# A fused attention, expert and feed-forward kernel: the order of its attention part is changed

## The chip, the cores and the metric

The kernel runs on one core of a Trainium2 chip. The metric is the device time of one execution in microseconds (us); lower is better. Engines are named as in the profile: PE (TensorE matmul) and PEld (its weight load), DVE (VectorE), ACT (ScalarE), POOL (GpSimd), SP (SyncE, which here only issues transfers). A name with a q behind it (ACTq, SPq) is the engine's instruction queue: issuing a transfer shows there.

## What is computed

Three stages follow one another: a decayed linear attention over 2 sequences of 768 tokens (8 heads of 64), a mixture of 8 experts in which each of the 1536 tokens goes to the 2 best by a noisy gate, and a dense feed-forward with a softmax-like activation and a norm.

```python
# attention: q, k, v of (2, 8, 768, 64)
gamma = 1.0 - 2.0 ** (-5.0 - np.arange(H, dtype=np.float32))
for t in range(S):
    state = gamma[None, :, None, None] * state + np.einsum('bhd,bhe->bhde', k[:, :, t], v[:, :, t])
    y[:, :, t] = scale * np.einsum('bhd,bhde->bhe', q[:, :, t], state)
# experts: x of (1536, 512), 8 experts of 512 x 1024 x 512
logits = x @ w_gate
noise_scale = np.log1p(np.exp(x @ w_noise))
noisy_logits = logits + noise_scale * noise
top2 = np.argpartition(-noisy_logits, 2, axis=1)[:, :2]
for e in range(E):
    for k in range(2):
        mask = top2[:, k] == e
        h = np.maximum(x[mask] @ w1[e], 0.0)
        out[mask] += top2_w[mask, k, None] * (h @ w2[e])
# feed-forward: 512 -> 1024 -> 512
h = x @ w_in
solu = h * softmax(h)
ln = (solu - mu) / np.sqrt(var + 1e-06) * g_ln
return ln @ w_out
```

## The kernel before, in words

**Attention.** 12 tiles of 128 tokens, one a step (i = 0 to 11; tiles of the two sequences in turn). A step issues on PE: `from_state` (L407, the query against the running state), `kv` (L418, the state's update), `from_chunk` (L433, within the tile), `scores(i + 1)` (L390), and `rows_logits(i)` (L444: the tile's rows and its 16 gate columns, out of the tile's transposed result `xT`). DVE masks the scores (`pm`, L392), ACT copies out the state `S` (L422), `xT` (L435), the rows `x` (L448) and the logits (L449). POOL scales queries and values two steps ahead (`qs`, L374, and `vs`, L378). SP issues the loads of queries, keys and values three steps ahead (`load_qk`, `load_kv`: four of 256 KB a tile), the store of the rows to `xd` (256 KB, L450) and, in seven of the steps, a load of 512 KB of the first expert's weights (`feed`); `split_unit` turns these into two parts on ACT (L202) and DVE (L203).

**Choosing.** The tiles are chosen in groups of 4, 4, 2 and 2. `choose(g)`, driven by `route(g)`, is a chain of some 25 small DVE operations (L466 to L489) with one trip to ACT; its `chosen` (L481) and `cum` (L483) are what `rank(g)` multiplies on PE (L561, L562) to number the tokens of each expert. `first_rows` (L503 to L513) makes from it the list of the first expert's tokens; `slots` (L571 to L579) makes the places in the table `token_of`; `scatter(i)` writes tile i's token numbers there with two indirect transfers on POOL (L629, L630). All 24 of them must have landed before POOL reads the second expert's list (`load_xg(1)`, L899) and gathers its rows `xr` in four indirect transfers (L914).

**First expert.** `list_rows` and `first_xt` gather its rows directly. `hidden(0, f, ...)` (L645) first computes 192 tokens for f = 0 to 7, then, after `turns` (order of the experts, and the list addresses `at_r`, L593), the other 256. `second(0, j)` (L969) follows in four pieces of 24 matmuls; behind the first piece PE turns the second expert's rows (`xg_t(1, 0)`, L928), and so on. From there on PE works through the experts and the feed-forward.

**Order.** The order is written out by hand: each engine and each queue runs its instructions in the order of the program, and waits on semaphores at the head. At the start ACT's queue issues two loads (`dec`, `kt`), then eleven small transfers: zeros to the table, eight pieces of 64 partitions x 2 x 8 numbers of the gates, written straight into `unit` (L280), the noise in two (L284), `gcol` (L286); its first computation (`fade`, L352) stands behind them. The pools give three buffers each to the loaded tiles, to `qs`, `vs` and `x`.

Of the kernel before, what the change touches and what calls it, by code (L numbers as in the profile page):

```python
# [44 lines left out]
def retnet_moe_solu(ctx, tc, qT, kT, k, v, w_gate, w_noise, noise, w1, w2, w_in, w_out, g_ln,  # L45
# [195 lines left out]
    def load_kv(i):  # L241
        if i >= NT:
            return
        c, b = order[i]
        for src, dst, nm in ((v, VT, "vt"), (k, KN, "kn")):
            t = ld.tile([128, H, D], F32, tag=nm, name=nm)
            nc.sync.dma_start(t, src[b, c])
            dst[i] = t
# [3 lines left out]
    load_qk(0)  # L252
    load_kv(0)
# [16 lines left out]
    nc.scalar.dma_start(token_of[:E * ROOM].rearrange("(p n) o -> p (n o)", p=128), zero)  # L270
# [3 lines left out]
    gate_at = (slice(128, 128 + 2 * E), slice(0, 2 * E))  # L274
# [8 lines left out]
    for b in range(B):  # L283
# [53 lines left out]
    load_kv(2)  # L337


    rows = [bank("c2", (128, HP, 128)), bank("c3", (128, HP, 128))]  # L340
# [6 lines left out]
    for s in range(2):  # L347
# [6 lines left out]
    first = wk.tile([128, 128], F32, name="first", bufs=1)  # L354
    nc.vector.memset(first, 0.0)
    nc.vector.memset(first[0:1], math.sqrt(D))
    p = bank("a1", (128, NC, H))
    nc.tensor.matmul(p, first, dec[:, 1], start=True, stop=True)
    chunk = wk.tile([128, NC, HP], F32, name="chunk", bufs=1)
    for s in range(2):  # L360
        r = slice(64 * s, 64 * s + 64)
        nc.vector.tensor_copy(chunk[r], p[r, :, s::2])
# [5 lines left out]
    def scale_qv(i):  # L368
# [12 lines left out]
    def scores(i):  # L381
# [56 lines left out]
    def rows_logits(i):  # L438
        x = wk.tile([128, 2, 2, 2, D], F32, tag="x", name="x", bufs=3)
# [231 lines left out]
    for i in range(NT):  # L671
        load_qk(i + 3)
        load_kv(i + 3)
# [3 lines left out]
        from_chunk(i)  # L677
        if i == 10:
            list_rows(0, range(EARLY_TILES), "a0")
        scores(i + 1)  # L680
        if i == 5:
            rank(0, "a1")
        rows_logits(i)
        if i == 4:
            route(0)
# [5 lines left out]
        if i == 7:  # L691
            slots(0)
        if i == 8:
            route(1)
            route(1)
            scatter(0)
            rank(1, "a1")
        if i == 9:
            first_rows(1)
            scatter(1)  # L700
        if i == 10:
            route(1)
            slots(1)
            scatter(2)
            route(2)
        if i == 11:
            route(2)
            scatter(3)
            rank(2, "a1")
            first_xt(0, 0)  # L710
            route(2)
            first_xt(0, 2)
            first_rows(2)
        feed(max(0, min(i - 3, LEAD)), max(0, min(i - 1, LEAD + 3)))
# [527 lines left out]
```

## Time and profile before

| what | value |
|---|---|
| time of the runs | 571.66, 572.23, 574.74 us (median 572.23) |
| the profiled execution: its time, its span | 572.88 us, 570.9 us |
| PE busy | 516.4 us (90%) |
| DVE, ACT, POOL busy | 373.3, 216.8, 232.8 us |
| mean granted clock of TensorE | 0.952 |
| PE in 40 slices (tenths) | 7598578882999999999999999999799888999986 |
| PE's clock in 40 slices (tenths) | 9798895995999999999999999999989899999999 |

A slice is 14.3 us; a 9 means busy for 90% or more. The first ten slices hold the attention, the choosing and the first expert. A row of a timeline gives the start and the length in us, the engine, the line, the operation, the tile written and those read, and in brackets how long the engine had been idle and what released it. A length is that of one instruction, or from the first start to the last end where x counts more.

### The profile page before, as it was taken

The numbers are of one execution on the slowest core, as the hardware profiler recorded it, in microseconds if no ns is written. First come the engines' busy times: TensorE is split into PE (matmuls) and PEld (weight loads), VectorE is DVE, ScalarE is ACT, GpSimd is POOL, SyncE is SP. The second block draws the span as 40 slices with busy tenths as digits, with TensorE's granted clock in tenths as the row PEclk, the third lists the DMA queues.
The fourth block names the chain that finished last, engine by engine and source line by source line (L and its number), as shares of the span: only waits on it lengthen the run. The fifth ranks groups of instructions, "written<-read, shape, count | busy, mean of one in ns | idle before, by whom it ended". The sixth has DMA issues, their size and how long they took to land.

```text
span 570.9 us, 8942 instructions
## 1 busy us (share of the span) xinstructions
PE 516.4 (90%) x3211; PEld 467.4 (82%) x3211; DVE 373.3 (65%) x731; ACT 216.8 (38%) x430; POOL 232.8 (41%) x309
## 2 busy tenths in 40 slices
PE   7598578882999999999999999999799888999986
PEld 6587467881999899999999999998587767878776
DVE  4139665550777888698787988885357566565640
ACT  0565331331443243343433425434434443334431
POOL 3436540775666572460714500000423545553421
PEclk9798895995999999999999999999989899999999
DMA  6699722205866668587686775758433553555331
GB/s 230 168 301 351 275 69 90 75 2 166 282 214 184 210 212 280 159 232 235 211 215 217 184 264 182 209 150 235 141 101 71 170 148 121 162 144 158 99 95 58
DMA packets 60514, 100.88 MB, mean 177 GB/s; under 512 B 11024, under 2 KB 28528, under 8 KB 60464
## 3 DMA queue, kind: packets, MB, share of 16 engines
q1 hardware_dynamic: 49680, 84.30, 47.2%
q0 software_dynamic: 6592, 15.54, 9.4%
q10 hardware_dynamic: 4192, 0.41, 0.5%
q8 instruction: 27, 0.44, 0.3%
q14 instruction: 23, 0.19, 0.1%
HBM read 77.52 MB, written 22.70 MB: 176 GB/s over the span
## 4 chain that ended last, share of the span: by engine, by line
PE 52%; DVE 12%; DMA 5%; ACT 4%; issue 3%; POOL 0%; SPq 0%; POOLq 0%; ACTq 0%; DVEq 0%
PE c L969 18%; PE b L645 11%; PE a L645 11%; PE d L767 7%; PE b L854 4%; DVE z L786 2%; DVE ee L781 2%; DVE t L739 2%; ACT ee L780 1%; DVE st L772 1%; DMA wr<-w_out 1%; PE a L748 1%; DMA zc<-zd 1%; DVE wl L203 1%; DMA xr<-xd,rows 1%
## 5 line engine op out<-in xcount | busy, mean ns | idle before, releaser
L914 POOL DMA_INDIRECT xq<-xd,rows x78 | 85.4, 1095 | 61.8 <-issue 61.1
L203 DVE TENSOR_TENSOR wl<-wr,wh 128x1024 fp32r<-128x1024 f32 x68 | 81.8, 1220 | 2.5 <-ACT wh L202 2.4
L969 PE MATMUL c<-hh,wh 128*128 128x448 f32 (+5 forms) x224 | 79.9, 357 | 0.0
L969 PE MATMUL c<-hl,wh 128*128 128x448 f32 (+5 forms) x224 | 79.6, 355 | 0.0
L969 PE MATMUL c<-hh,wl 128*128 128x448 f32 (+5 forms) x224 | 79.5, 355 | 0.0
L202 ACT ACTIVATE wh<-wr 128x1024 fp32r<-128x1024 f32 x68 | 70.0, 1051 | 1.2 <-DMA wr<-in_moe_w_dram 1.2
L728 POOL DMA_INDIRECT y<-yg,slot_y x24 | 23.8, 993 | 91.4 <-DMA yg<-y 85.8
L645 PE MATMUL b<-xh,wh 128*128 128x192 f32 (+8 forms) x176 | 58.3, 341 | 2.8 <-DVE hl L648 1.3
L645 PE MATMUL b<-xh,wl 128*128 128x192 f32 (+8 forms) x176 | 57.3, 335 | 0.0
L844 POOL TENSOR_TENSOR zl<-zc,zh 128x1024 fp32r<-128x1024 f32 x10 | 24.2, 2422 | 50.1 <-ACT zh L843 50.1
L969 PEld LDWEIGHTS c<-hh,wh 128*128 128x128 f32 x224 | 42.8, 191 | 1.2
L969 PEld LDWEIGHTS c<-hh,wl 128*128 128x128 f32 x224 | 42.6, 190 | 1.2
L969 PEld LDWEIGHTS c<-hl,wh 128*128 128x128 f32 x224 | 42.6, 190 | 1.2
L767 PE MATMUL d<-wh,x2h 128*128 128x512 f32 x96 | 40.3, 420 | 1.5 <-ACT y L1034 1.5
L647 ACT ACTIVATE hh<-b 128x192 fp32r<-128x192 f32 (+8 forms) x44 | 20.0, 454 | 54.5 <-PE b L645 51.2
L854 PE MATMUL b<-wh,zh 128*128 128x512 f32 (+1 forms) x104 | 38.4, 375 | 1.5 <-ACT zh L843 1.5
L767 PE MATMUL d<-wh,x2l 128*128 128x512 f32 x96 | 39.4, 411 | 0.0
L767 PE MATMUL d<-wl,x2h 128*128 128x512 f32 x96 | 39.0, 407 | 0.0
L645 PEld LDWEIGHTS b<-xh,wh 128*128 128x128 f32 x176 | 35.4, 201 | 4.4 <-DVE hl L648 1.7
L645 PE MATMUL a<-xh,wh 128*128 128x448 f32 (+6 forms) x112 | 38.9, 348 | 0.0
L645 PE MATMUL a<-xh,wl 128*128 128x448 f32 (+6 forms) x112 | 38.8, 346 | 0.0
L854 PE MATMUL b<-wl,zh 128*128 128x512 f32 (+1 forms) x104 | 38.3, 374 | 0.0
(206 smaller groups left out, 1087.0 us busy)
## 6 DMA issues: line engine op xcount, KB each, us to landing
wr<-in_moe_w_dram SPq DMA_DIRECT2D x60, 512.0 KB, 5.6
zd<-zs SPq DMA_DIRECT2D x40, 128.0 KB, 2.3
zc<-zd SPq DMA_DIRECT2D x10, 512.0 KB, 4.2
raw<-in_moe_w_in_dram SPq DMA_DIRECT2D x8, 512.0 KB, 4.7
raw<-in_moe_w_out_dram SPq DMA_DIRECT2D x8, 512.0 KB, 4.8
yg<-yr SPq DMA_DIRECT2D x16, 208.0 KB, 3.8
qt<-in_qT_dram SPq DMA_DIRECT2D x12, 256.0 KB, 5.3
vt<-in_v_dram SPq DMA_DIRECT2D x12, 256.0 KB, 5.5
```

The source lines that it names most:

```text
L202: nc.scalar.activation(hi, t, AF.Copy)
L203: nc.vector.tensor_sub(lo, t, hi)
L645: nc.tensor.matmul(p, w[:, 0, f * 128:(f + 1) * 128], x[:, d, c], start=(n == 0), stop=(n == len(terms) - 1))
L647: nc.scalar.activation(hh[:, f, c], p, AF.Relu)
L728: nc.gpsimd.indirect_dma_start(out=t, out_offset=None, in_=yg[:upto], in_offset=bass.IndirectOffsetOnAxis(ap=slot_y[:, i, s:s + 1], axis=0))
L739: nc.vector.scalar_tensor_tensor(t, y1, top_w[:, i, 1:2], t, op0=OP.mult, op1=OP.add)
L767: nc.tensor.matmul(PH[i][:, s, :], x[:, c], w[:, 0, f], start=(n == 0), stop=(n == 3 * KD - 1))
L781: nc.vector.scalar_tensor_tensor(ee, ph, 1.0, ee, op0=OP.mult, op1=OP.mult, accum_out=col(2))
L844: nc.gpsimd.tensor_sub(lo, t, hi)
L854: nc.tensor.matmul(p, z[:, f * 128:(f + 1) * 128], unit_t[8 * E + 4 + f // 2][n][:, f % 2, c], start=(m == 0), stop=(m == len(terms) - 1))
L914: nc.gpsimd.indirect_dma_start(out=x[:, b] if e > 1 else xr_t[e][b], out_offset=None, in_=src[:], in_offset=bass.IndirectOffsetOnAxis(ap=r ...
L969: nc.tensor.matmul(py[d][:, :CAPS[e]], c, h[:, f, :CAPS[e]], start=(f == 0 and n == 0), stop=(f == KF - 1 and n == 2))
```

## The change

- ACT's queue at the start keeps `dec`, `kt` and two transfers that load both gates into a tile `wgn`; eight small copies on DVE put them into `unit`. Noise, zeros and `gcol` go to SP's queue, behind the loads of the first three tiles and ahead of the fourth tile's values and keys, which are loaded before the loop. A one-column copy makes ACT load its table first.
- The mask is made within the first step's scores, half by half, and the small matmul for `chunk` stands behind these scores.
- `rank(0)`, `rank(1)`, `rank(2)` stand in steps 6, 9 and 11 (before: 5, 8 and 11), ahead of that step's `rows_logits`; `route(0)` is spread over steps 4, 5 and 7.
- `scatter` runs for two tiles a step (four transfers) in steps 8 to 11, and for the last four tiles within the first expert's first half, as soon as their slots are there; `slots(2)` is in the attention's last step.
- The loaded values and keys get four buffers; `qs`, `vs` and `x` get two.
- `feed` runs two steps earlier: weights are loaded from step 0 and split from step 2.

```diff
-            t = ld.tile([128, H, D], F32, tag=nm, name=nm)
+            t = ld.tile([128, H, D], F32, tag=nm, name=nm, bufs=4)
...
+    wgn = wk.tile([128, KD, 2 * E], F32, name="wgn", bufs=1)
+    nc.scalar.dma_start(wgn[:, :, :E], w_gate.rearrange("(k p) e -> p k e", p=128))
+    nc.scalar.dma_start(wgn[:, :, E:], w_noise.rearrange("(k p) e -> p k e", p=128))
...
-    nc.scalar.dma_start(token_of[:E * ROOM].rearrange("(p n) o -> p (n o)", p=128), zero)
...
-        for n, w in enumerate((w_gate, w_noise)):
-            for j in range(2):
-                at = gate_at[half].start + E * n
-                nc.scalar.dma_start(unit[64 * j:64 * j + 64, :, half, at:at + E],
-                                    w.rearrange("(k j s p) e -> k j p s e", k=2, j=2, s=2)[half, j])
...
-        nc.scalar.dma_start(nz[:, b:NT:B, :], noise[b * S:(b + 1) * S, :].rearrange("(c p) e -> p c e", p=128))
...
-    nc.scalar.dma_start(gcol, g_ln.rearrange("(k p) -> p k", p=128))
...
+    for b in range(B):
+        nc.sync.dma_start(nz[:, b:NT:B, :], noise[b * S:(b + 1) * S, :].rearrange("(c p) e -> p c e", p=128))
+    nc.sync.dma_start(token_of[:E * ROOM].rearrange("(p n) o -> p (n o)", p=128), zero)
+    nc.sync.dma_start(gcol, g_ln.rearrange("(k p) -> p k", p=128))
+    load_kv(3)
+
+
+    nc.scalar.activation(part[:, 2:3], part[:, 2:3], AF.Copy)
...
-            t = wk.tile([128, HP, 128], F32, tag="qs", name="qs", bufs=3)
+            t = wk.tile([128, HP, 128], F32, tag="qs", name="qs")
...
-            t = wk.tile([128, H, D], F32, tag="vs", name="vs", bufs=3)
+            t = wk.tile([128, H, D], F32, tag="vs", name="vs")
...
         for s in range(2):
+            if not i:
+                make_mask(s)
             nc.vector.tensor_mul(t[:, s], p[s], mask[:, s])
+        if not i:
+            gates()
...
-        x = wk.tile([128, 2, 2, 2, D], F32, tag="x", name="x", bufs=3)
+        x = wk.tile([128, 2, 2, 2, D], F32, tag="x", name="x")
...
+        scores(i + 1)
+        if i == 6:
+            rank(0, "a1")
+        if i == 9:
+            rank(1, "a1")
...
+        if i == 11:
+            rank(2, "a1")
         rows_logits(i)
...
         if i == 8:
+            scatter(0)
+            scatter(1)
             route(1)
             route(1)
-            scatter(0)
-            rank(1, "a1")
...
-        feed(max(0, min(i - 3, LEAD)), max(0, min(i - 1, LEAD + 3)))
+        feed(max(0, min(i - 1, LEAD)), max(0, min(i + 1, LEAD + 3)))
...
         if f == 0:
             route(3)
             route(3)
+            scatter(8)
+            scatter(9)
...
-            slots(2)
             route(3)
             slots(3)
-        if f in (3, 4, 5, 6):
-            for i in (4 + 2 * (f - 3), 5 + 2 * (f - 3)):
-                scatter(i)
+            scatter(10)
+            scatter(11)
```

**ACT at the start of the program, before** (`fade` is its first computation; the lines of after are some 10 to 20 higher):

```order
L251 DMA dec<-in_decay_dram 128x96
L238 DMA kt<-in_kT_dram 128x512
L270 DMA token_of<-zero 128x32
L280 DMA unit<-in_moe_w_gate_dram 64x2x8 x2
L280 DMA unit<-in_moe_w_noise_dram 64x2x8 x2
L284 DMA nz<-in_moe_noise_dram 128x6x8 x2
L286 DMA gcol<-in_moe_g_ln_dram 128x8x1
L352 ACT_TABLE_LOAD
L352 ACTIVATE fade<-c_239 64x512
```

and now:

```order
L251 DMA dec<-in_decay_dram 128x96
L238 DMA kt<-in_kT_dram 128x512
L254 DMA wgn<-in_moe_w_gate_dram 128x4x8
L255 DMA wgn<-in_moe_w_noise_dram 128x4x8
L338 ACT_TABLE_LOAD
L338 ACTIVATE part<-part 128x1
L356 ACTIVATE fade<-c_239 64x512
L356 ACTIVATE fade<-c_240 64x512
L433 ACTIVATE S<-a_255,chunk 128x64 x4
L446 ACTIVATE xT<-c_309 128x256
```

Eleven small transfers ahead of the first computation have become two, and the state's copies `S` follow.

**PE at the end of step 8, before**: the scores of step 9 (L390), the rows of step 8 (L444), then the second group's rank (L561, L562), which reads `chosen` and `cum`:

```order
L390 MATMUL b<-qt,kt 128x128 x8
L444 MATMUL c_1002<-unit,xT 128x144 x2
L444 MATMUL c_1008<-unit,xT 128x144 x2
L561 LDWEIGHTS before
L561 MATMUL a_1046<-chosen,before 128x32
L562 LDWEIGHTS ones
L562 MATMUL a_1046<-cum,ones 128x32
L407 MATMUL c_1053<-qs,S 64x128 x2
L407 MATMUL c_1054<-qs,S 64x128 x2
```

**PE now**, a step later: `from_chunk` and the scores of step 10 (L444, L397), the rank (L572, L573), then the rows of step 9 (L455):

```order
L444 MATMUL c_1058<-pm,vt 64x128 x4
L444 MATMUL c_1059<-pm,vt 64x128 x4
L397 MATMUL b<-qt,kt 128x128 x8
L572 LDWEIGHTS before
L572 MATMUL a_1105<-chosen,before 128x32
L573 LDWEIGHTS ones
L573 MATMUL a_1105<-cum,ones 128x32
L455 MATMUL c_1109<-unit,xT 128x144 x2
L455 MATMUL c_1115<-unit,xT 128x144 x2
```

The same rank stands one step further back on PE; on DVE its choice stands behind the mask of step 9's scores in both.

**DVE within the first expert's first half, before** (f = 3: `hl` is a hidden block's low part, L571 to L579 are the third group's slots, L486 begins the fourth group's):

```order
L648 SCALAR_TENSOR_TENSOR hl<-b,hh 128x192
L531 CAST rows_176<-a_1372 128x2
L571 TENSOR_TENSOR pk<-pk,a_1278 128x32
L572 TENSOR_REDUCE ranks<-pk 128x4
L574 TENSOR_SCALAR sets<-ranks 128x4
L575 SCALAR_TENSOR_TENSOR rt<-top_i,ranks 128x2x2
L576 SCALAR_TENSOR_TENSOR rt<-sets,rt 128x2x2
L578 SCALAR_TENSOR_TENSOR rt<-ranks,behind 128x2x2
L579 SCALAR_TENSOR_TENSOR slot<-rt 128x4
L486 MAX_INDEX ix<-top,rt 128x8 x2
```

**DVE now**, at the end of the attention's last step, ahead of the first expert's first `hl`:

```order
L524 TENSOR_SCALAR oh<-col,s_1315 128x256 x2
L497 MAX_INDEX ix<-top,rt 128x8 x2
L498 CAST top_i<-ix 128x4
L500 TENSOR_TENSOR pk<-e_161,top_i 128x32
L582 TENSOR_TENSOR pk<-pk,a_1276 128x32
L583 TENSOR_REDUCE ranks<-pk 128x4
L585 TENSOR_SCALAR sets<-ranks 128x4
L586 SCALAR_TENSOR_TENSOR rt<-top_i,ranks 128x2x2
L587 SCALAR_TENSOR_TENSOR rt<-sets,rt 128x2x2
L589 SCALAR_TENSOR_TENSOR rt<-ranks,behind 128x2x2
L590 SCALAR_TENSOR_TENSOR slot<-rt 128x4
L739 MEMSET mhalf 128x1
```

The third group's index search and slots moved from the middle of the first expert's first half to ahead of it.

## Rows read from the trace of the kernel before

**Rows 1.** Timeline of TensorE, first and second expert (start us, length us, engine, line ... [idle before])

```profile
87.56 0.53 PE L645 MATMUL b<-xh,wh 128*128 128x192 f32 x1 [0.84 <-DVE xl L552]
...
126.29 0.37 PE L969 MATMUL c<-hh,wl 128*128 128x448 f32 x1
...
140.35 0.47 PE L928 MATMUL a<-ident,xr 128*128 128x128 f32 x1 [1.72 <-DMA xr<-xd,rows]
```

**Rows 2.** Timeline of GpSimd, the last scatter, the list's read and the last gather

```profile
126.00 0.96 POOL L630 DMA_INDIRECT token_of<-token,slot  x1 [0.23 <-issue]
...
128.89 0.97 POOL L899 DMA_INDIRECT rows<-token_of,at_r  x1 [1.93 <-issue]
...
135.77 0.95 POOL L914 DMA_INDIRECT xr<-xd,rows  x1 [0.31 <-issue]
```

**Rows 3.** Groups of instructions by line, 0 to 145 us (busy us, mean ns | idle before)

```profile
L630 POOL DMA_INDIRECT token_of<-token,slot x24 | 26.0, 1082 | 5.1 <-issue 4.9 <-DVE lg L466 0.2
```

**Rows 4.** Timeline of VectorE, the last slots and the list addresses

```profile
104.46 0.19 DVE L579 SCALAR_TENSOR_TENSOR slot<-rt 128x4 uint32<-128x4 f32 x1
...
111.50 0.15 DVE L593 SCALAR_TENSOR_TENSOR at_r<-turn,part 128x1 uint32<-128x1 f32 x1
```

**Rows 5.** Chain of waits, in order of time (start us, length us, what)

```profile
140.82 6.85 PE c L969 x24
...
148.11 4.86 PE c L969 x24
```

**Rows 6.** Timeline of all engines, first 21 us

```profile
6.70 0.34 ACTq L270 DMA_DIRECT2D token_of<-zero  x1
...
8.98 0.42 PE L358 MATMUL a<-dec,first 128*128 128x48 f32 x2 [1.75 <-DVE first L356]
...
15.15 1.12 ACTq L286 DMA_DIRECT2D gcol<-in_moe_g_ln_dram  x1
...
16.31 1.28 ACT L352 ACT_TABLE_LOAD   x1 [16.31 <-DMA qt<-in_qT_dram]
...
20.09 2.29 PE L444 MATMUL c<-unit,xT 128*128 128x144 f32 x8 [6.47 <-ACT xT L435]
```

**Rows 7.** Timeline of TensorE, attention steps 3 to 9

```profile
30.70 1.25 PE L444 MATMUL c<-unit,xT 128*128 128x144 f32 x8
...
31.88 0.67 PE L407 MATMUL c<-qs,S 64*64 64x128 f32 x16
...
35.06 1.25 PE L444 MATMUL c<-unit,xT 128*128 128x144 f32 x8
...
45.52 0.18 PE L561 MATMUL a<-chosen,before 128*128 128x32 bf16 x1 [1.68 <-DVE chosen L481]
...
67.59 0.19 PE L561 MATMUL a<-chosen,before 128*128 128x32 bf16 x1 [5.65 <-DVE chosen L481]
...
68.30 1.13 PE L407 MATMUL c<-qs,S 64*64 64x128 f32 x16
...
73.74 1.25 PE L444 MATMUL c<-unit,xT 128*128 128x144 f32 x8
```

**Rows 8.** Timeline of TensorE, end of the attention

```profile
85.64 0.17 PE L561 MATMUL a<-chosen,before 128*128 128x16 bf16 x1 [1.47 <-DVE chosen L481]
```

**Rows 9.** Timeline of VectorE, second group's choice

```profile
60.79 1.29 DVE L392 TENSOR_TENSOR pm<-b,mask 128x512 f32<-128x512 f32 x2 [0.45 <-PE b L390]
...
66.40 1.13 DVE L481 TENSOR_TENSOR chosen<-rt,top 128x32 bf16<-128x32 f32 x1
```

**Rows 10.** Engines in stretches (busy us (instructions) by engine, PEclk, DMA share, GB/s)

```profile
40.00:49.00 9.00, 6.91 (x92) 5.96 (x94) 8.05 (x27) 4.63 (x22) 5.04 (x4) 0.83 1.03 394
...
50.00:62.00 12.00, 11.94 (x188) 10.24 (x183) 10.92 (x28) 8.62 (x36) 7.18 (x5) 1.00 0.98 342
...
87.00:101.00 14.00, 11.71 (x76) 11.53 (x77) 6.93 (x37) 1.77 (x7) 0.00 (x0) 0.52 0.21 74
```

**Rows 11.** The stores of the attention's rows, tile x

```profile
DMA to landing us min/median/max: 2.0/3.5/6.4
```

More of the change, by code (lines that the diff above doesn't have):

```diff
@@ L273, in retnet_moe_solu @@
     unit = wk.tile([128, 2, 2, 128 + 2 * E], F32, name="unit", bufs=1)
-    gate_at = (slice(128, 128 + 2 * E), slice(0, 2 * E))
     for half in range(2):
         nc.vector.tensor_copy(unit[:, :, half, 2 * E * half:2 * E * half + 128], ident[:, None, :].to_broadcast([128, 2, 128]))
-        for n, w in enumerate((w_gate, w_noise)):
-            for j in range(2):
-                at = gate_at[half].start + E * n
-                nc.scalar.dma_start(unit[64 * j:64 * j + 64, :, half, at:at + E],
-                                    w.rearrange("(k j s p) e -> k j p s e", k=2, j=2, s=2)[half, j])
     nz = const.tile([128, NT, E], F32, name="nz")
-    for b in range(B):
-        nc.scalar.dma_start(nz[:, b:NT:B, :], noise[b * S:(b + 1) * S, :].rearrange("(c p) e -> p c e", p=128))
     gcol = const.tile([128, KF], F32, name="gcol")
-    nc.scalar.dma_start(gcol, g_ln.rearrange("(k p) -> p k", p=128))
     e8 = const.tile([128, E], F32, name="e8")
@@ L346, in retnet_moe_solu, with make_mask @@
                              start=(hp == 0), stop=True, skip_group_check=True)
-    for s in range(2):
+    first = wk.tile([128, 128], F32, name="first", bufs=1)
+    nc.vector.memset(first, 0.0)
+    nc.vector.memset(first[0:1], math.sqrt(D))
+    chunk = wk.tile([128, NC, HP], F32, name="chunk", bufs=1)
+    def make_mask(s):
         for hp in range(HP):
@@ L352, in retnet_moe_solu, with gates @@
         nc.scalar.activation(fade[r], rows[s][r], AF.Copy)
[L354 to L362, printed above, removed]
+    def gates():
+        p = bank("a1", (128, NC, H))
+        nc.tensor.matmul(p, first, dec[:, 1], start=True, stop=True)
+        for s in range(2):
+            r = slice(64 * s, 64 * s + 64)
+            nc.vector.tensor_copy(chunk[r], p[r, :, s::2])
+        for half in range(2):
+            for s in range(2):
+                for j in range(2):
+                    at = 128 * (1 - half)
+                    nc.vector.tensor_copy(unit[64 * j:64 * j + 64, s, half, at:at + 2 * E], wgn[64 * s:64 * s + 64, 2 * half + j, :])
     S_bufs = {}
@@ L672, in retnet_moe_solu @@
         load_qk(i + 3)
-        load_kv(i + 3)
+        if i:
+            load_kv(i + 3)
         scale_qv(i + 2)
@@ L677, in retnet_moe_solu @@
         from_chunk(i)
+        scores(i + 1)
[3 more added lines that the diff above has]
+            rank(1, "a1")
         if i == 10:
             list_rows(0, range(EARLY_TILES), "a0")
-        scores(i + 1)
-        if i == 5:
-            rank(0, "a1")
+        if i == 11:
+            rank(2, "a1")
         rows_logits(i)
         if i == 4:
-            route(0)
             route(0)
@@ L691, in retnet_moe_solu @@
         if i == 7:
+            route(0)
             slots(0)
         if i == 8:
+            scatter(0)
+            scatter(1)
             route(1)
             route(1)
-            scatter(0)
-            rank(1, "a1")
         if i == 9:
             first_rows(1)
-            scatter(1)
-        if i == 10:
+            scatter(2)
+            scatter(3)
             route(1)
             slots(1)
-            scatter(2)
+        if i == 10:
+            scatter(4)
+            scatter(5)
+            route(2)
             route(2)
         if i == 11:
-            route(2)
[L708 to L713, printed above, removed]
-        feed(max(0, min(i - 3, LEAD)), max(0, min(i - 1, LEAD + 3)))
+            first_xt(0, 0)
+            first_xt(0, 2)
+            scatter(6)
+            scatter(7)
+            first_rows(2)
+            route(2)
+            slots(2)
+        feed(max(0, min(i - 1, LEAD)), max(0, min(i + 1, LEAD + 3)))
     att.close()
```

## Prediction, made before the changed kernel had run

> **What bounds the kernel now.** PE is busy for 90% of the span, so I looked for the places where it waits. The slices of PE are thin at the start (7, 5 tenths), at the fifth and sixth (5, 7), and thinnest at the tenth (2); from the eleventh on they are nearly solid, and it is the same code in both kernels. The chain of waits, read backwards, leaves PE only at the second expert's first rows, so that place comes first; then the timeline of PE from the start to that place, and for each hole the timeline of the engine that ends it.
>
> The largest hole: PE ends the first piece of `second(0)` at 126.29 + 0.37 = 126.66 and is released for the last transpose of the second expert's rows at 140.35 [rows 1]. Those rows come from POOL: the last scatter issues until 126.96, the read of the list follows at 128.89, the four gathers end with the one issued at 135.77 [rows 2]. A scatter costs POOL (26.0 + 5.1) / 24 = 1.3 us [rows 3]; the last 16 of the 24 stand in its queue behind two gathers of the first expert's second half, begin about when the fourth group's slots are written, at 104.65 [rows 4], and fill POOL for some 21 us, until 126.96. So POOL's queue, not the arithmetic, sets this wait. After it TensorE is at the lower of its clock levels: the next 24 matmuls take 6.85 us, the 24 behind them 4.86 [rows 5].
>
> The second hole is at the start: PE stands still for 6.47 us before 20.09, waiting for `xT` [rows 6]. ACT could not make it: its queue issues small transfers from 6.70 to 16.27, and only then loads its table, at 16.31 [rows 6]. (The profile names a load as the releaser there; the queue's own rows show the issues.) Then three waits for `chosen`: 1.68, 5.65 and 1.47 us [rows 7, 8].
>
> **The price of the clock.** A step at full clock lasts 35.06 - 30.70 = 4.36 us. From its first block (L407) to L444 it takes 35.06 - 31.88 = 3.18; after the hole before 67.59 the same blocks take 73.74 - 68.30 = 5.44 [rows 7]. So a hole that lets the clock fall costs some 2.3 us more than itself.
>
> **Start.** Eleven small transfers on ACT become two. ACT's table load and `fade` then stand behind two issues, and `S` and `xT` follow as soon as PE has them; `rows_logits(0)` stands on PE right behind `scores(1)`, where the 6.47 us were. That wait goes. The mask's halves now stand between the scores' halves on DVE, and the wait of 1.75 us before `chunk`'s matmul at 8.98 [rows 6] mostly moves behind the scores; I take 0.9 of it as gained (0 to 1.75). The clock's 2.3 go too. Gain: 6.5 + 0.9 + 2.3 = 9.7. New on the way are the two loads of `wgn` and eight copies on DVE. No row shows a load of that shape; the nearest are the small transfers here, the last of which issues until 16.27, so the bound is 0 (it lands while the masks are made) to all of the 6.5 (it lands as late as they do). I take 0: it is issued third, ahead of everything that delayed the others. The copies stand ahead of the mask of the second scores, which PE needs only after `rows_logits(0)`. On SP the noise, zeros and `gcol` now stand ahead of the fourth tile's loads, which PE needs three steps, some 13 us, later.
>
> What the row shows here is an issue queue that costs its engine 9.6 us [rows 6]. The Trainium skill (DMA: Bandwidth & Descriptors, section Issuing engines are not separate DMA queues) says that transfers from all issuing engines run on the same DMA engines and that spreading them saves only the sequencer's time, usually small. By its "usually small" the start would gain next to nothing, and the sum below would lose 9.7; by the row it is the whole wait. I follow the row.
>
> **Ranks.** Group 1: its second half of the choice runs in step 5 on DVE, and PE asks for it at the end of the scores in step 6, a step later than those; the 1.68 us [rows 7] and the clock's 2.3 go: 4.0 (bounds 0 and 4.0, since the first half needs a place on DVE too). Group 2: on DVE, mask, choice and `chosen` run from 60.79 to 67.53 = 6.7 us behind the scores [rows 9]. PE now comes to the rank one step, 4.36, after these scores, so it waits 6.7 - 4.4 = 2.4, instead of 5.65: gain 3.3. The wait remains, and with it the clock's fall: no 2.3 here. Group 3: its rank now stands ahead of `rows_logits(11)` and behind more DVE work (the second group's slots are ahead of its choice, as before); it waited 1.47 [rows 8] and loses the cover of one block, 1.25 us [rows 7]. `xT` no longer stands behind it on ACT. I take 0, between -1.3 and +1.5. Ranks: 7.3.
>
> **First expert's first half.** DVE gets the third group's slots ahead of the first `hl` (later `hl`: a small loss) and loses them in the middle (a small gain). I take 0, from -1 to +1. PE works here at a clock of 0.52 for 11.7 us [rows 10]; at full clock, by 3.18 to 5.44, that is 4.9 less, of which the wait for the fourth group's rank would take part: 0 to 4.9, and I take 0.
>
> **Scatters.** Count from the first matmul of the first expert, T = 87.56 [rows 1]. The fourth group's slots are ready at T + 17.1, the list's address `at_r` at 111.65 = T + 24.1 [rows 4]. In the new order four scatters (5.2 us) stand behind the gathers and these slots instead of 16, so they end at T + 22.3; allowing the 1.93 us that the list's read waited behind the last scatter [rows 2], it starts at T + 24.2, as `at_r` does. From that read to the last landed gather took 140.35 - 128.89 = 11.5 [rows 1, 2]: T + 35.7. PE needs it at 126.66 = T + 39.1. So 3.4 us to spare, and the hole goes whole: 140.82 - 126.66, less 0.45 for four transposes = 13.7, plus 6.85 - 4.86 = 2.0 for the clock [rows 1, 5]: **15.7**. The scatters before these: 20, of which even the last 12, if none had started by T, would end at T + 15.6, ahead of the fourth group's slots. Four a step (5.2) are more than a step (4.36), but POOL has no `vs` left then; what stands behind them is `qs(11)` and the first two gathers of the first expert's rows, which I price at 0 to 3 us late and take as 0. What is late next, behind the hole: the second expert's weights, which POOL issues behind the gathers; they move forward with them.
>
> **Loads and buffers.** A step that loads weights moves four loads and a store of 256 KB and 512 KB of weights: 1.84 MB. In the busiest stretch the transfers ran at 394 GB/s, in a long one beside a running loop at 342 [rows 10]: 4.7 or 5.4 us against 4.36. Weights start two steps earlier and no wait separates the steps now, so over seven steps the loads fall behind by 2.1 to 7.1 us. They run three steps ahead, which covers some 5: price 0 to 2, and I take 0. Fewer buffers for `qs` and `vs` tie POOL to PE two steps back, 8.7 us, for one instruction each. `x` with two buffers waits for the store of two steps before: it lands in at most 6.4 us [rows 11]; of the two steps' 8.7 the emptying of the banks and SP's queue leave some 7, by my estimate. Four buffers for values let SP issue half a step earlier; I take 0.
>
> **Sum.** 9.7 + 7.3 + 15.7 = 32.7 us off the profiled execution's 572.88 (span 570.9 and 1.98 around it): 540.2. That execution is 0.65 above the median of the runs, so 540 to the nearest microsecond. All that follows the second expert's rows is unchanged and PE-bound, and shifts as a whole.
>
> **Rivals.**
> 1. *The loads pace the attention.* At the slower rate the loop falls 7.1 behind and the cover is spent by the waits that are gone: 3 to 7 us back, 543 to 547, or more if the idle gaps also lower the clock. For it: DMA share 0.98 to 1.03 [rows 10]. Against: the cover. The Trainium skill (DMA: Bandwidth & Descriptors, section Specifications) puts HBM's share of one core at about 358 GB/s, which would speak for this case; the 394 of rows 10 is above it. By its figure a step takes 5.1 us and the time would be some 543. Chance 0.15.
> 2. *The hole at the second expert stays in part.* POOL falls behind: late gathers of the first expert's rows, then late scatters, then the list. Half of the 15.7 stays: 548. For it: four scatters a step are longer than a step. Against: 3.4 us to spare. Chance 0.12.
> 3. *The clock stays up in the first expert*: up to 5 less, 535. Chance 0.1.
> 4. *The transfers are not what held ACT or PE*, and the change doesn't do at the start what it says: 9.7 come back, 550. Chance 0.05.
> 5. *Slower than before*: the two buffers of `x`. If a store under full load lands later than the 7 us, ACT waits in every step before it may empty the rows' banks, PE idles in every step, and the clock never returns: a step would take 4.36 x 5.44 / 3.18 = 7.5, 3.1 more in each of 11 steps = 34, more than the 32.7: about 574, and beyond 575 with the waits themselves. It decides from a landing of 7 us on in nearly all steps; the longest is 6.4 [rows 11]. Chance 0.03.
>
> **How the numbers follow.** Forecast 540 with chance 0.55, own range 536 to 544. Rivals as above. The range that holds 8 in 10 takes in the forecast's own, rival 1, rival 3 and most of rival 2: 532 to 549. A difference of 0.5% (about 3 us) is about what a measurement of this kernel can tell from none. Faster by more: all but rival 5, 0.96; within: 0.01; slower: 0.03.
>
> **What would show it.** In the profile of the changed kernel: `rows_logits(0)` starting on PE at about 13 (not 20); step 1 to 8 at 4.36 without waits (rival 1: waits for loads or `qs` among them); a wait of 2 to 3 us at the second group's rank; the first expert's first matmul at about 70 to 71; the list's read right behind `at_r`, and no wait of PE at the second expert's transposes. A PE wait there, a clock of 1.2 GHz in the loop, or ACT waiting for the store of `x` would make the prediction wrong.

## The result, and the profile after

The changed kernel took 540.81 us, the median of four runs (537.62 to 545.66), the kernel before 573.28 beside it (571.66 to 574.74): ratio 0.944, 95% interval 0.936 to 0.952. Two more comparisons of the same kernel gave 539.98 (0.950, 0.943 to 0.957) and 540.61 (0.943, 0.939 to 0.947). Forecast were 540.0 and a range of 532 to 549.

The first profiled execution of the changed kernel is the longest of its four runs, 545.66 us with a span of 543.7. Two later ones have spans of 539.2 and 540.6. The table sets three places on PE side by side (us from the span's start): the second `rows_logits`, the first hidden matmul of the first expert (T), and the third piece of the second expert, which is the first one that neither the hole nor the clock behind it touches.

| | before | after, first | after, second | after, third | forecast gain | measured gain |
|---|---|---|---|---|---|---|
| `rows_logits(1)` | 26.34 | 18.01 | 18.36 | 17.43 | 9.7 | 8.0 to 8.9 |
| from there to T | 61.22 | 57.19 | 53.85 | 56.01 | 7.3 | 4.0 to 7.4 |
| T to the third piece | 60.55 | 46.67 | 46.31 | 46.63 | 15.7 | 13.9 to 14.2 |
| third piece to the end | 422.8 | 421.8 | 420.7 | 420.5 | 0 | 1.0 to 2.3 |
| span | 570.9 | 543.7 | 539.2 | 540.6 | 32.7 | 27.2 to 31.7 |

The page of the first execution: PE's busy tenths and the granted clock in 40 slices. The slice of 2 tenths that stood tenth before is gone; what is left thin lies between the fourth and the seventh slice.

```profile
span 543.7 us, 8943 instructions
...
PE   8998758899999999999999999999798999999996
...
PEclk9998897899999999999999999999799999999999
```

The start, on ACT (timeline: start, us, instruction, idle time ahead of it and its releaser). The rows answer to ACT's in [rows 6]: four issues, the table's load at 2.84 instead of 16.31, and `xT` of the first step at 12.61.

```profile
2.28 0.53 ACTq L255 DMA_DIRECT2D wgn<-in_moe_w_noise_dram  x1
2.84 1.28 ACT L338 ACT_TABLE_LOAD   x1 [2.84 <-issue]
...
12.61 0.67 ACT L446 ACTIVATE xT<-c 128x256 f32<-128x256 f32 x2
```

PE of the same execution, where it waited (timeline). These rows answer to [rows 1, 6 to 8]: the wait for `xT` has become two short ones for the gate weights' copies. Of the three waits for `chosen` (L572) and `cum` (L573) none is gone: the first is as long as it was (2.2 us with `cum`, before 2.1), the second is 3.2 us instead of 6.1, the third 2.19 instead of 1.47. The fourth group's, at 82.42, is 4.30 us; before it was 1.71. Before the third one PE had waited for `xT` too, 1.62 us, and that wait is gone. The two rows of before:

```profile
82.93 1.25 PE L444 MATMUL c<-unit,xT 128*128 128x144 f32 x8 [1.62 <-ACT xT L435]
...
94.71 0.17 PE L561 MATMUL c<-chosen,before 128*128 128x16 bf16 x1 [1.71 <-DVE chosen L481]
```

The rows after the change:

```profile
11.49 0.66 PE L444 MATMUL c<-pm,vt 128*64 128x128 f32 x8 [1.17 <-DVE pm L401]
13.84 0.48 PE L455 MATMUL c<-unit,xT 128*128 128x144 f32 x2 [0.60 <-DVE unit L369]
14.50 1.00 PE L455 MATMUL c<-unit,xT 128*128 128x144 f32 x6 [0.17 <-DVE unit L369]
18.01 1.25 PE L455 MATMUL c<-unit,xT 128*128 128x144 f32 x8
22.37 1.25 PE L455 MATMUL c<-unit,xT 128*128 128x144 f32 x8
...
42.36 0.18 PE L572 MATMUL a<-chosen,before 128*128 128x32 bf16 x1 [1.81 <-DVE chosen L492]
42.95 0.18 PE L573 MATMUL a<-cum,ones 128*128 128x32 bf16 x1 [0.41 <-DVE cum L494]
58.61 0.18 PE L572 MATMUL a<-chosen,before 128*128 128x32 bf16 x1 [0.98 <-DVE chosen L492]
61.00 0.19 PE L573 MATMUL a<-cum,ones 128*128 128x32 bf16 x1 [2.21 <-DVE cum L494]
72.16 0.17 PE L572 MATMUL a<-chosen,before 128*128 128x16 bf16 x1 [2.19 <-DVE chosen L492]
75.20 0.36 PE L656 MATMUL b<-xh,wh 128*128 128x192 f32 x1 [0.88 <-DVE xl L563]
82.42 0.17 PE L572 MATMUL c<-chosen,before 128*128 128x16 bf16 x1 [4.30 <-DVE chosen L492]
96.35 0.98 PE L558 MATMUL a<-ident,xr 128*128 128x128 f32 x7 [1.79 <-DMA xr<-xd,rows]
...
115.97 0.60 PE L947 MATMUL a<-ident,xr 128*128 128x128 f32 x4
```

The last row answers to the 13.7 us in [rows 1]: the second expert's transposes start with no wait. POOL shows why (timeline): the last scatter is issued by 97, and the list's read, which stood behind it in [rows 2], now waits 3.27 us for DVE's `short`, next to the list's address; from T to `at_r` (99.87) it is 24.7 us, where it was 24.1 [rows 1, 4].

```profile
95.92 0.96 POOL L641 DMA_INDIRECT token_of<-token,slot  x1 [0.22 <-issue]
100.15 0.97 POOL L918 DMA_INDIRECT rows<-token_of,at_r  x1 [3.27 <-DVE short L606]
```

### The profile page after: what moved, and what is told of

The parts are those of the page before. It is cut to its first block, busy times and chain, and to the rows that moved or that the text cites. A ratio compares the mean times of both kernels' runs of the same rounds, so it can differ in the third digit from the quotient of the medians.

```text
span 543.7 us, 8943 instructions
## 1 busy us (share of the span) xinstructions
PE 508.6 (94%) x3211; PEld 461.9 (85%) x3211; DVE 379.0 (70%) x739; ACT 216.0 (40%) x431; POOL 233.2 (43%) x309
## 4 chain that ended last, share of the span: by engine, by line
PE 68%; DVE 16%; DMA 6%; ACT 5%; issue 3%; POOL 1%; SPq 0%; DVEq 0%; ACTq 0%; POOLq 0%
PE c L988 20%; PE b L656 14%; PE a L656 11%; PE d L786 8%; PE b L873 6%; DVE z L805 3%; PE c L455 2%; DVE ee L800 2%; DVE t L758 2%; DMA wr<-w_out 1%; PE b L397 1%; DVE st L791 1%; ACT ee L799 1%; DVE wl L203 1%; PE a L767 1%
## 5 line engine op out<-in xcount | busy, mean ns | idle before, releaser
L203 DVE TENSOR_TENSOR wl<-wr,wh 128x1024 fp32r<-128x1024 f32 x68 | 83.2, 1244 | 5.0 <-ACT wh L202 5.0
L863 POOL TENSOR_TENSOR zl<-zc,zh 128x1024 fp32r<-128x1024 f32 x10 | 24.7, 2465 | 47.9 <-ACT zh L862 47.9
L953 ACT ACTIVATE xh<-xt 128x428 fp32r<-128x428 f32 (+5 forms) x24 | 13.0, 540 | 64.2 <-DVE xt L951 64.2
```

The source lines that it names most:

```text
L203: nc.vector.tensor_sub(lo, t, hi)
L863: nc.gpsimd.tensor_sub(lo, t, hi)
L953: nc.scalar.activation(hi, t, AF.Copy)
```

## Experiments

**The same kernel again.** Is the first execution's lag of 4.9 us on the median in the attention or behind it? No edit.

> The changed kernel, unchanged, in another execution. The first profiled execution took 545.7 us where the median of the runs is 540.8. Theory 1: the spread lies in the attention, where DVE's small operations run into POOL's: then in an execution of about 540 the first expert's first matmul starts at 70 to 72 us of the span instead of 75.2 and the rest is the same. Theory 2: the spread lies behind the second expert's rows: then that matmul stands at 75 +- 0.5 again and the stretch from the third piece of the second expert (121.87 in the first execution) to the end is not 421.8 but some 417.

539.98 us; the profiled execution took 540.97, with T at 72.21 instead of 75.20. From the third piece on it is 1.1 shorter. Theory 1 holds for 3.0 of 4.5 us of span. Behind the first rank the two executions part (a stretch and its length, the busy time of PE, PEld, DVE, ACT and POOL with their counts, then granted clock, DMA share and GB/s; the first line is of the first execution, the second of this one):

```profile
44.00:49.00 5.00, 5.00 (x68) 4.10 (x67) 3.76 (x10) 2.40 (x12) 3.64 (x4) 0.69 1.04 381
```

```profile
44.00:49.00 5.00, 5.00 (x96) 4.25 (x90) 4.97 (x19) 2.62 (x14) 3.37 (x4) 1.00 1.05 385
```

In the first, PE waited 1.81 + 0.41 us for the rank and the clock fell to its lower level for a while; in the second it waited 1.13 + 0.42 and the clock stayed.

**The scatters back.**

```
         if i == 8:
             scatter(0)
-            scatter(1)
...
-            slots(2)
...
         if f == 3:
...
+            slots(2)
             route(3)
             slots(3)
-            scatter(10)
-            scatter(11)
+        if f in (3, 4, 5, 6):
+            for i in (4 + 2 * (f - 3), 5 + 2 * (f - 3)):
+                scatter(i)
```

> The changed kernel with the scatters and the third group's slots where they were. The recorded theory: POOL's queue sets the list's read again, PE waits 12 to 14 us for the second expert's rows and the clock falls behind it: +14 to +16 us against the changed kernel, about 555. Rival: the list's address and the gathers set that wait, not the scatters ahead of them: 0 to +3 us, 541 to 544.

557.56 us, 17.6 above the run of the changed kernel beside it, somewhat more than the 14 to 16 expected. PE's timeline and its chain of waits:

```profile
122.23 0.45 PE L942 MATMUL a<-ident,xr 128*128 128x128 f32 x1 [7.50 <-DMA xr<-xd,rows]
123.77 0.48 PE L942 MATMUL a<-ident,xr 128*128 128x128 f32 x1 [1.09 <-DMA xr<-xd,rows]
124.95 0.48 PE L942 MATMUL a<-ident,xr 128*128 128x128 f32 x1 [0.70 <-DMA xr<-xd,rows]
127.22 0.47 PE L942 MATMUL a<-ident,xr 128*128 128x128 f32 x1 [1.79 <-DMA xr<-xd,rows]
```

```profile
127.69 6.18 PE c L983 x24
133.88 0.44 PE a L942 x4
134.31 4.87 PE c L983 x24
```

11.1 us of waiting are back, with 1.3 of clock behind them: T to the third piece takes 58.0. POOL's list read stands 1.92 us behind its last scatter again. The rest of the difference is a T of 76.28, where this execution's second rank waited 4.84 us. That wait has to do with the scatters too: with two transfers in step 8 instead of four, POOL's next `qs` begins at 56.30, amid the second group's choice, and seven of its small operations take 3.25 us; in the three executions of the changed kernel this `qs` begins at 58.8 to 59.5, behind them, and they take 1.55 to 1.59 (why such operations stretch is the subject of the run with POOL's products twice). The rival (0 to 3) is out.

**The start back.** The eleven small transfers on ACT's queue, the masks' new place kept.

```
+        for n, w in enumerate((w_gate, w_noise)):
+            for j in range(2):
+                at = 128 * (1 - half) + E * n
+                nc.scalar.dma_start(unit[64 * j:64 * j + 64, :, half, at:at + E],
+                                    w.rearrange("(k j s p) e -> k j p s e", k=2, j=2, s=2)[half, j])
...
-                    nc.vector.tensor_copy(unit[64 * j:64 * j + 64, s, half, at:at + 2 * E], wgn[64 * s:64 * s + 64, 2 * half + j, :])
```

> The changed kernel with the noise, the zeros, the column of gains and the gate weights as eleven small transfers on ACT's queue again; the order of the masks and everything else as changed. The recorded theory (ACT is held by issuing them): PE waits 6 to 7 us for xT of the first step again, rows_logits(0) at 20 us: +8 to +9.7, about 549. Rival: it was the place of the masks that counted: +0 to +1 us, about 541, with rows_logits(0) at 13 to 15.

549.07 us, +9.1. ACT's timeline, then PE's:

```profile
16.56 0.75 ACTq L285 DMA_DIRECT2D gcol<-in_moe_g_ln_dram  x1
17.33 1.28 ACT L340 ACT_TABLE_LOAD   x1 [17.33 <-DMA unit<-in_moe_w_noise_dram]
```

```profile
21.20 1.09 PE L452 MATMUL c<-unit,xT 128*128 128x144 f32 x3 [9.02 <-ACT xT L443]
```

The second `rows_logits` starts at 26.45, where it was 26.34 in the kernel before: the place of the masks gives nothing by itself; the issues on ACT were the cause. Where the profile names a load as the table's releaser, the queue's rows ahead of it show what ACT did meanwhile.

**The ranks back.** `rank(0)` in step 5 and `rank(1)` behind the choice in step 8, and the first group's choice whole in step 4.

> The changed kernel with the ranks of the first two groups asked for a step earlier, as before (and the first group's choice whole in one step). The recorded theory: +7.3 us (4.0 for the first group with the clock, 3.3 for the second), about 548. Theory from the trace of the changed kernel, in which both ranks still wait (2.2 and 3.2 us) and the clock still falls behind them: the first group's term is near 0 and only the second group's wait grows back to 5 to 6 us: +2 to +3, about 543.

544.56 us (540.88 to 547.63), +4.6: between the two theories, nearer to the second, and its scatter covers both ends. Its trace shows waits of 2.64 + 0.41 and 4.39 + 0.42 us at the two ranks and T at 77.24, 2.0 to 5.0 later than in the three executions of the changed kernel. The time alone doesn't settle it: the interval (0.953 to 0.966) overlaps that of the changed kernel beside it (0.943 to 0.957), and this execution's span, 539.0 us, is as short as the changed kernel's second, because what lies behind T was 5 us shorter here.

**POOL's products twice.** Why does the first rank still wait? In the second execution of the changed kernel DVE's rows and POOL's read thus (timelines; `rt` are the choice's small tiles, and the last two of POOL's rows fall around the start of the choice's second half, at 38.76):

```profile
33.39 1.22 DVE L480 SCALAR_TENSOR_TENSOR rt<-rt 128x32 f32<-128x32 f32 x1 [0.43 <-ACT rt L478]
34.64 0.96 DVE L481 TENSOR_SCALAR rt<-rt 128x32 f32<-128x32 f32 x1
35.63 0.87 DVE L485 SCALAR_TENSOR_TENSOR rt<-rt 128x32 f32<-128x32 f32 x4
...
37.56 1.28 DVE L401 TENSOR_TENSOR pm<-b,mask 128x512 f32<-128x512 f32 x2
38.76 1.66 DVE L485 SCALAR_TENSOR_TENSOR rt<-rt 128x32 f32<-128x32 f32 x3
40.45 0.19 DVE L486 SCALAR_TENSOR_TENSOR rt<-rt 128x32 f32<-128x32 f32 x1
```

```profile
33.28 1.28 POOL L381 TENSOR_TENSOR qs<-qt,fade 128x512 f32<-128x512 f32 x1 [1.27 <-DMA qt<-in_qT_dram]
34.52 1.04 POOL L385 TENSOR_TENSOR vs<-vt,dec 128x512 f32<-128x512 f32 x1
37.86 1.28 POOL L381 TENSOR_TENSOR qs<-qt,fade 128x512 f32<-128x512 f32 x1 [2.30 <-DMA qt<-in_qT_dram]
39.10 1.04 POOL L385 TENSOR_TENSOR vs<-vt,dec 128x512 f32<-128x512 f32 x1
```

The first two of DVE's, in the first execution, where POOL's `qs` begins only behind them, at 33.87:

```profile
33.30 0.19 DVE L480 SCALAR_TENSOR_TENSOR rt<-rt 128x32 f32<-128x32 f32 x1 [0.29 <-ACT rt L478]
33.53 0.18 DVE L481 TENSOR_SCALAR rt<-rt 128x32 f32<-128x32 f32 x1
```

An operation of 0.19 us takes 1.22 or 0.96 when it meets a product of POOL's, and ends within 0.05 us of it. The three operations at 38.76, 0.65 us at the pace of the four at 35.63, took 1.66 here and 2.33 in the first execution: 1.0 and 1.7 us too long, against waits of 1.13 and 1.81 us for `chosen`. So the products were doubled:

```
-            nc.gpsimd.tensor_mul(t, QT[i], fade)
+            for n in range(2 if i in (6, 7) else 1):
+                nc.gpsimd.tensor_mul(t, QT[i], fade)
...
```

The product for `vs` is doubled in the same way.

> The changed kernel with POOL's two products of the steps 4 and 5 made twice (2.3 us more of POOL in each; same values). Theory: a small operation of DVE on two SBUF operands, and others, that meets a product of POOL lasts until it ends (1.2 instead of 0.2 us), which is where the first group's 4.0 us went: the choice takes 1 to 4 us longer, the rank waits 3 to 5 us instead of 1.55 to 2.2, and the time is +2 to +6. Rival: DVE's long operations have another cause (its own queue, ACT, the loads): the choice keeps its length, the rank its wait, +-1 us, unless PE waits for vs itself.

The second half of the choice, from its first operation to the start of `cum`, took 7.0 us instead of 3.0, and the rank's two matmuls came at 44.98 and 47.37 instead of 41.78 and 42.37. Two of the rows: 0.19 us became 1.15 and 0.97, and both end with a product.

```profile
41.66 1.15 DVE L489 TENSOR_TENSOR rt<-rt,nz 128x32 f32<-128x32 f32 x1
42.84 0.97 DVE L490 TENSOR_TENSOR rt<-rt,lg 128x32 f32<-128x32 f32 x1
```

PE's wait at the rank itself was 2.77, less than expected, since PE had waited 1.10 and 1.46 for the doubled products just ahead. The stretching is shown, and that it delays the rank. One thing more stands between the halves of the choice, a split `wl` of 1.22 us on DVE; no run took that out. The time, 568.2 (0.971), I don't use: this kernel, the next, the first of the one on buffers and the scatters alone were measured on a chip on which the kernel before took 586 us, and in their traces ACT stands 3 to 11 us for releases that the trace doesn't name, from step 11 on. These four are read by their stages ahead of that, and what lies behind it with reserve.

**The weights' feed back** (`feed(i - 3, i - 1)` as before).

> The changed kernel with the weights of the first expert loaded and split two steps later, as before. The question is why the rank of the first group still waits (1.55 and 2.2 us in two executions). Theory a (the weights' splits on DVE, 1.2 us each, now stand ahead of and between the halves of the choice): the waits don't change much, since splits then stand in steps 4 to 7 and still in the same two steps: 0 to -1 us. Theory b (loads compete with qT and so delay POOL's products into the choice): POOL's waits for qt go, and the rank's wait with its clock falls by 2 to 4 us. Recorded: 0.

0.949 (0.935 to 0.963). The first rank waited 0.98 + 0.41 us at 40.98; POOL still waited 2.8, 2.3 and 1.4 us for `qt` of three tiles around it. The run separates neither theory from the other: with the feed two steps later weights are still loaded in these steps (at 33.69 and 38.24, with a DMA share of 1.05 from 35 to 45 us), and a split `wl` still stands between the halves of the choice. The rank's 1.39 us lie within the spread of the executions (0.96 to 2.22). Whether the loads delay POOL's products into the choice stays open.

**The buffers back** (three for values, keys, `qs` and `x`, and the fourth tile's values and keys loaded within the loop again), twice.

> The changed kernel with three buffers for values and keys (loaded as before), three for qs and for x. The recorded theory: buffers are worth 0, within +-3 us of the changed kernel. Rival: the fourth buffer is what lets the steps run at 4.36 without waits (or qs and x with two cost something): +3 to +6, with PE waiting for vt, kn or vs in steps 3 to 8.

0.956 (0.942 to 0.969) on the chip of the 586 us, where it tells nothing; so once more:

> The changed kernel with three buffers for values and keys, for qs and for x, once more: in the first run of it the kernel before took 586 us instead of 570 to 573, and ACT and PE stood for several us behind releases that the trace can't name, so that its ratio (0.956, 0.942 to 0.969) tells nothing. Recorded theory: buffers are worth 0: 0.943 to 0.950 of the kernel before, 539 to 543. Rival: +3 to +6, 0.950 to 0.957, with PE waiting for vt, kn or vs in steps 3 to 8.

542.26 us, 0.946 (0.941 to 0.951), and no wait of PE for `vt`, `kn` or `vs`. The price of 0 holds, within 3 us.

**The scatters alone**, in the kernel before.

> The kernel before with the scatters' part of the change alone (four scatters a step from step 8, the third group's slots in step 11). The recorded theory: the hole at the second expert's rows goes whole without the rest of the change: -14 to -17 us against the kernel before, and PE doesn't wait at those transposes. Rival: four scatters a step hold up qs or the gathers of the first expert's rows in this slower loop and take part of it back: -7 to -12.

574.44 beside 586.27: 0.980 (0.966 to 0.994), or -11.8 with an interval of some +-8: not settled by its time. In the trace the second expert's pieces follow one another without a wait at the transposes; but ACT's `hh` of the first expert stood 10.91 us for one of those unnamed releases, and PE then waited 10.46 us at the fourth group's rank: it came later by that, so the missing wait at the transposes proves little here.

**A better order.** If the waits left over are waits for DVE, what needs no rank soon can wait longer, and the fourth group's choice can go first:

```
         scores(i + 1)
+        if i == 10:
+            list_rows(0, range(EARLY_TILES), "a0")
+        rows_logits(i)
         if i == 6:
             rank(0, "a1")
         if i == 9:
             rank(1, "a1")
-        if i == 10:
-            list_rows(0, range(EARLY_TILES), "a0")
-        if i == 11:
-            rank(2, "a1")
-        rows_logits(i)
...
-            first_rows(2)
-            route(2)
-            slots(2)
+            rank(2, "a1")
+            route(3)
+            route(3)
...
         if f == 0:
-            route(3)
-            route(3)
+            first_rows(2)
+            route(2)
+            slots(2)
```

(`list_rows(1, ...)` moves one piece later.) The changed kernel ran beside it:

> The changed kernel once more, as the measure for the two kernels beside it: 0.944 to 0.95 of the kernel before, about 540 us, the first expert's first matmul between 72 and 75.5 us of the span and a wait of 4.2 to 4.3 us at the fourth group's rank.

540.61 us, 0.943, T at 73.44, the fourth rank's wait 4.60.

> The changed kernel with the ranks of the first two groups behind rows_logits of their step (not ahead of it), the third group's rank behind the first expert's transposes, and the fourth group's choice on DVE ahead of the third group's first_rows, list part and slots. Theory: what is left of the ranks is waiting for DVE and can be covered: 1.25 us each at the first two, 2 to 3 of the 4.2 at the fourth with up to 3 of clock behind it: -4 to -8 against the changed kernel, 532 to 536. Rival: DVE is full in these steps and hands the wait on to pm, xl or hl: 0 to -2.

534.64 us (532.77 to 535.69), 0.934 (0.930 to 0.937): 6.0 below the changed kernel, and the fastest of all. The waits at the third and fourth rank are gone; T to the third piece takes 42.85 instead of 46.63, T itself hardly moved (73.00), because the gathers of the first expert's rows now end PE's wait there:

```profile
41.67 0.18 PE L572 MATMUL a<-chosen,before 128*128 128x32 bf16 x1 [0.30 <-DVE chosen L492]
57.80 0.18 PE L572 MATMUL a<-chosen,before 128*128 128x32 bf16 x1 [1.08 <-DVE chosen L492]
71.36 0.80 PE L558 MATMUL b<-ident,xr 96*128 96x96 f32 x7 [1.77 <-DMA xr<-xd,rows]
```

Between the two traced executions lie 7.0 us of span: 0.4 up to T, 3.8 from T to the third piece, and 2.8 behind it, where nothing was changed; the spread of that last stretch (416.6 to 422.8 over these runs) is larger.

**And one step further**: the first two tiles' scatters behind `qs(11)`, and four copies of the gate weights instead of eight.

> As the kernel ahead of it, with four copies of the gate weights instead of eight on DVE (385 ns each) and the first two tiles' scatters behind qs of the last tile on POOL. Theory (small operations of DVE pay for meeting POOL's products): another -0.8 at the start, where PE waits 0.6 + 0.2 for the copies, and 0 to -1.8 at the second group's rank: -1 to -2.5 against the kernel ahead of it. Rival: the wait for pm of 1.17 ahead of it takes the place, and the scatters are late for the list: 0 to +2.

539.51 us, 0.944: 4.9 slower than the kernel ahead of it, on the rival's side and beyond its +2. The list of the first expert's rows was written at 65.07, but four scatters moved behind `qs(11)` stood in POOL's queue until 66.8; the gathers were issued at 67.15 and 68.41 instead of 65.71 and 66.98, and PE waited 2.42 and 3.44 us for them. 1.4 of that is the queue; why the gathers then took longer to land isn't shown. The copies gave 0.24: four of 64x32 took 2.48 us, eight of 64x16 3.08.

## Why the prediction was right, and where its terms were off

**Start, 9.7: right, a little too high.** 8.0 to 8.9 in three executions, 9.1 by undoing it. ACT's queue was the cause. The step that was mis-sized is "copies stand ahead of the mask of the second scores, which PE needs only after `rows_logits(0)`": `rows_logits(0)` itself needs them, they take 3.08 us on DVE, and PE waited 0.7 to 1.0 for them in the three executions. They take so long because two of the eight meet POOL's products and take 0.95 and 0.99 us (first execution); the median copy takes 0.17. Of the 1.75 that I counted at 0.9, 1.17 stayed as a wait for `pm`. The Trainium skill (DMA: Bandwidth & Descriptors, Issuing engines are not separate DMA queues) calls the sequencer's time "usually small relative to the DMA itself". For one issue the trace of the kernel before agrees: the eight pieces of the gates took 0.6 to 0.9 us each to issue and 3.2 to 3.4 (medians) to land. But eleven such issues held ACT for 9.6 us [rows 6], and that was worth 8.0 to 9.1, because the first step's work stood behind them on the same engine.

**Ranks, 7.3: too high, by the first group's term.** The path from `rows_logits(1)` to T gained 4.0, 5.2 and 7.4 us; undoing two of the three ranks cost 4.6, with overlapping intervals. Cut at the fifth, eighth and eleventh `rows_logits`, the path shows where (us):

| | before | after: first, second, third | forecast gain | measured gain |
|---|---|---|---|---|
| fifth to eighth (group 1) | 16.92 | 17.76, 15.30, 14.89 | 4.0 | -0.8, 1.6, 2.0 |
| eighth to eleventh (group 2) | 22.11 | 18.28, 17.40, 18.70 | 3.3 | 3.8, 4.7, 3.4 |
| eleventh to T (group 3) | 9.12 | 8.08, 8.08, 9.35 | 0 | 1.0, 1.0, -0.2 |

Group 1's 4.0 was taken at its upper bound: the wait was to vanish, and it stayed at 1.0 to 2.2 us. In the first execution the clock fell behind it (0.69 from 44 to 49 us, so in part at 1.2 GHz), which I had named as a sign of being wrong; there this group lost time. What I left out is that the choice on DVE and the products on POOL block each other; the two halves now stand beside products in two steps. Group 2's rank was to wait 2.4 us and waited 2.2 to 3.6. Group 3's rank waited 2.2 instead of 1.5, but the wait of 1.6 for `xT` ahead of it went, as I had argued.

**First half, 0: wrong by some 1.6.** T to the third piece was to take 60.55 - 15.7 = 44.85 and took 46.3 to 46.7. From T to the fourth rank it takes 7.1 to 7.5 us, as before (7.15): the first two pieces ran at full clock, as rival 3 had it, but what that gave went into the rank's wait, 4.2 to 4.6 us instead of 1.7. DVE had the third group's slots, 1.1 to 1.3 us, newly ahead of the fourth choice; I had called their move "a small loss". In the run with scatters and slots put back the wait is 3.12. The 1.6 us were lost behind that rank. The clock was low there, as before (0.50 to 0.56 over the next six us; before, 0.51). Then PE waited 1.79 and 1.64 us for the gathers of the first expert's second half in the first and third execution, for which it had not waited before; in the second the clock stayed at 0.50 from 85.3 to 92.3, where the kernel before, as far behind its rank, had it at 1.00. In the better order T to the third piece takes 3.8 us less than in the changed kernel beside it.

**Scatters, 15.7: right for the hole.** The hole is gone with its clock, and the list's read stands behind `at_r`: from the end of the first piece to the third takes 5.7 us instead of 21.5. Putting the scatters back costs 11.1 us of wait and 1.3 of clock in the trace, 17.6 in the median. Counted as in the prediction, the hole that comes back is 127.69 - 114.73 - 0.45 = 12.5 us instead of 13.7: the list's read is issued 39.5 us behind T, where it was 41.3 [rows 1, 2]. T to the third piece grows by less, 11.4 to 11.7, since what lies between T and the end of the first piece is 2 us shorter with the third group's slots back in their old place (38.5, against 40.6 to 40.9 in the changed kernel and 39.1 before). By this one execution the move that closes the hole is also what costs the first half its 1.6.

**Loads and buffers, 0: right.** The steps between the second and the sixth `rows_logits` take 4.35 to 4.46 us with no load waited for on PE, while the DMA share was 1.0 or more. Behind the first rank transfers still ran at 381 and 385 GB/s (the two lines above); that is over the 358 GB/s for one core that rival 1 took from the Trainium skill (DMA: Bandwidth & Descriptors, Specifications). The cover did its work: POOL waited for `qt` 1.3 to 2.9 us in each step from 33 to 53 us of the first execution, PE did not. Rivals 1, 2, 4 and 5 are out. Rival 2's mechanism is real, though: the last kernel shows that POOL has no time to spare ahead of the first gathers. The late gathers of the second half are not its work: POOL stood idle for 4.02 us before the first of them, which waited for DVE.

**The total** is nearer than its terms, and that is in part luck. The three traced executions gained 27.2 to 31.7 us of span, not 32.7, and the three comparisons 29.9 to 32.5 us in the median. The terms that were too high (start 1, ranks 2, first half 1.6) add up to some 4.5, of which 1 to 2.3 came back behind the third piece, where nothing was changed. That is spread from one execution to the next: I saw 416.6 to 422.8 us for the same code.

## What to carry over

Look at the queue of the engine on which the first work stands: issues are work of that engine. Before pricing a wait at nothing, write out what stands ahead of it on the engine that ends it and which other engine's operations slow that one; where an engine answers several askers, let it give first the answer that is asked for first. Moving the fourth group's choice ahead of lists and slots that nobody waited for yet came with 3.8 us here; asking later at the first three ranks moved T by only 0.4, where the gathers' wait took the place of the third rank's. And where a queue has a deadline at either end, here the first gathers and the list's read, filling it earlier is safe only up to the first one.

## What the runs showed of the chip

- DVE's small operations on SBUF and POOL's products block each other for whole instructions. `rt` rows of 0.19 us took 0.96 to 1.22 and ended with POOL's product; `pm`, which reads one operand from PSUM, kept its 1.28 for two under the same products (second execution: 37.56 to 38.84, with `qs` from 37.86). It goes the other way too: `qs` took 2.32 instead of 1.28 where DVE's `wl` of 1.23 us had started 0.05 ahead of it (42.43 and 42.48, second execution). The Trainium skill (SBUF — State Buffer, Who interferes with whom) says that a DVE instruction with two SBUF inputs contends with a GpSimd instruction that reads SBUF, and that one in a 2-port mode and a GpSimd instruction share a port pair by an exclusive lock. These rows agree.
- The same holds for copies from SBUF to SBUF: of the eight of 64 partitions by 16 values six took DVE some 0.17 us each, and the two that met POOL's products 0.95 and 0.99. The copy of `chunk`, which reads PSUM, kept its 0.19 (at 11.53) beside the same `qs`.
- PE's wait of 2.2 us in all at a rank was followed by a granted clock of 0.69 over five us in one execution, one of 1.55 us in all by 1.00 in another.
